# Another order, with its engines and buffers, for the same pieces of an attention and MLP kernel

## The chip, the cores and the metric

The kernel runs on one core of one Trainium2 chip. The metric is the device time in microseconds (us) of one execution. The kernel before takes 614.69 us, the median of three runs (613.73 to 614.74).

## What is computed

```python
q, k = rotate(q), rotate(k)                      # rotary embedding, (4, 8, 576, 64)
scores = (1 / sqrt(64)) * q @ k.T
attn = exp(scores - max(scores)); attn = attn / (sum(attn) + 1e-9)
x = (attn @ v) as (2304, 512)                    # tokens x heads*64
h = x @ w_in                                     # (512, 2048)
out = (s * relu(h) ** 2 + b) @ w_out             # (2048, 512)
```

All inputs are of type float32; the weights are stored as 64-bit words and are turned into 32-bit numbers on the chip.

## The kernel before

The 32 heads are treated as 16 pairs (`NPAIR`), four of them for each of the four batches. Of each pair, q, k and v are loaded, q and k are rotated (`rotate`, three tensor-tensor steps each, lines 592, 594 and 596), scaled, split into two 16-bit parts (`qk_hi`, `qk_lo`, `v_hi`, `v_lo`) and transposed. The first four pairs (`FQ`) skip the split and are worked on in 32 bits. The scores of 128 rows form one tile: TensorE writes it to PSUM (`s_tile`, lines 675 and 676, or `s_pair`, line 657), VectorE takes the row maximum straight from PSUM (`s_max`, line 681), ScalarE the exponential (`s_exp`), and the normalised result is split into two halves `pab` (`p_a`, a scaled cast, and `p_b`, line 407). A DMA transposes `pab` into `pt` (`p_t`, line 739), and TensorE multiplies with v (`pv_sum`, line 760).

The 32 weight tiles are converted in four steps each (`w_sign`, `w_low`, `w_rebias`, `w_join`), and their largest column sums are taken (`w_gram`, line 478). Later they are split into two 16-bit halves in place (`w_hi`, `w_lo`). The MLP goes in nine units (`NU`). Unit 0 works in 32 bits (`mlp_in0`, line 913, `mlp_out0`, line 930), the others in three 16-bit products (`mlp_in`, line 887, `mlp_out`, line 963). A unit from 1 on begins with its norm: `x_norm` on ScalarE, two additions `x_add` (line 846), the matmul `x_sum` (line 852, one for each unit), then `x_scale`, `x_hi` and `x_lo`. After each first product come relu and square on ScalarE and a split into `g_hi` and `g_lo` (line 905). Unit 7 (`NU - 2`) is the last: its second half of rows is summed in two column halves, and `out_sum` and `store` follow for each of its three parts. Line 511 (`bias_cols`, 32 matmuls in a row) stands once in the program.

`plan()` lists 2691 pieces with what each reads and writes, and for some pieces the engines that may do them. Three tables of characters then fix everything else. `ORDER` gives the order in which the pieces are written, and so the order of every engine's queue. `PICKS` gives the engine of each piece that has a choice (G is GpSimd, S is ScalarE, V is VectorE). `SLOTS` gives the buffer that each new tile takes, of the few that `BUFS` allows (two for scores in PSUM, four for loaded weights, six for `pab`, two for `pt`). Each engine works through its queue in order, and all loads, transposes and stores stand in one queue, that of SyncE (SP). The loop that does it:

```python
for n in order:
    x = work[n]
    ...
    if x["pick"]:
        a = (*a, pick[x["fn"], a])
```

In the profile GpSimd is called POOL, VectorE DVE, ScalarE ACT and TensorE PE. Most VectorE and ScalarE steps go through helpers, so their line is that of the helper: 402 and 404 for a tensor-scalar step, 407 for `scalar_tensor_tensor` on VectorE, 410 for ScalarE.

Of the kernel before, what the change touches and what calls it, by code (L numbers as in the profile page):

```python
# [35 lines left out]


ORDER = (
    "AJADAGAFAEAHAKAMALANAOAIAPDUAADfEBECDgEDEEDhEFEGAdAeAfAgDVDWDkDTD_AhDcEHDdA3EADeDiEIA4EJDXA5DYDlESELDZDrDjA6A7EMEKJjJkEN"
# [3 lines left out]
    "EtK6KCBOBhLBJzLCKRFIBJBPE3BgFTBQBfFUKLBmEwKMBiK7BlLDB4B6B7KWBcBWKXKeCSACBnKDKSLEBoE4LFKEKYKZB5KaB8K8KfKTFhB-KbBjBpKnCVKg"
    "CUBqKhKvKoKwK9CTKcB_BdCWKdKiETClCLKUB9KjKpKqCBKVFVEqK-CACCKrKkLJCoLKLRFQKlCmKxCnLLKsKmLMKycdCMLSCNLTCpCOKzEUKtCPLNLrCDbM"
    "bObLLGCYK_FHCsCybNLULsCELVLWCZCaF7LHLOLtbPCbbQLICzC1LaLPK0CcbRExbSCXCdbTLXLQLuFkCuCvLiLbEyEzE0CtLcE1CwE-LdcecfcgCeLechE_"
    "ciMRLvFRLwLjC0LkLfMSLlC2CFC_DADBDCbWbVLYMTCICHLZLmE8bYF6L3bXK1KuCfCGLgL4MUbZbaL5F9DDMVcjCgCibhbgK2bfDMLnLxMEDODNMFCJLoLh"
# [39 lines left out]
PICKS = (
    "VSSGGGVSSGSSGSSGSSVSSGSSVVSGSSVSSGSGVSGGSSVVSVSGGSSGSSVSSGSSGSSVSSGSSGSSGSGGSSVSSGSGGSSGGGGGGGGSVVSSSVVSSSVVSSSVVSSSVVSS"
    "SVVSSSGVSSSVVSSSVVSSSVVSSSVVSGGVVGSVVVSSVGVGSGVVSVGVGGSSSSSVGSVGSSGSSGSSVSVGSSVSSSSSVGSGVSSGSSSSSVSSSSSGVSSSVSGVVSSGSSSS"
    "SSVSSSSSSSSSGGSSVSSSSGSSSSSSSSSSVSSSGSSSSSSSSSSSSSVVSSSGVSSSVSVSSVSVSSVVSVGVSGSSVSSSVSSSSSSSGSSSVVVVVSSGVSSSGSSSVSVGVSGG"
    "VGVSSSSSSGVSSSVSSVSSVVGVVVVVVSGVSGGVVGVVVVGVSSVSSVVGVSVVSSSSSSSSSGGSSGSSGSSGVSSVGSGSSGSGSVVSSVSGSGSVSGSGSVSGVSSGSVSVSGSG"  # L90
    "VVSGSVVVVGSGVGSVVGVGSGSGVSVVSGVGSVSVSGVVSGVVVVSVSVVGSVSGSVVVVVSVSVSGSGSVVGVGSGVVVGSGVVVGVVSVVVSVVVVGSVVGVVVGSGSGVV"
)

SLOTS = (
    "010000121000113110001201101002001331101011111210100101202011230001130011100330101010011021210131000112301100201031000121"
    "110131010323100010011223110113234005000101001201001112013401001312102101110500100031103241100310211030011000001303232140"
    "101412101013153012014011001101231020111130011054301130001001100112103122101540203010201100100013011031305400221101123301"
    "310010012401001113000011023110010020101053100120320101100110200111023300111010021001000510123101022112111300013110101104"
    "020200101200201103150010124011311210021031110011002510121100011230011010241101320050032110312010022000011130120010010101"
    "314111001011023502110002210013030410110005102011032001101001104220100001233115010013100121001301130014221111020113010105"  # L100
    "331000031010111500123010242010110103110000521421030100101242502102101100011201103130100112020030112330540011113001103120"
    "011321520121030040011201311003100200110013251402103120100013011010201012010002110210101254001002011310131012000012130110"
    "00221112000110020003013100110102111003201211001001311120100000101110210110001201010"
)


# [987 lines left out]
```

## Time and profile before

| | before |
|---|---|
| median of three runs | 614.69 us |
| span of the profiled execution, first to last instruction | 611.0 us |
| what lies around the span, against the median | 3.7 us |
| PE busy | 584.1 us, 96% of the span |
| DVE busy | 473.7 us, 78% |
| ACT busy | 412.8 us, 68% |
| POOL busy | 122.7 us, 20% |
| SP queue (loads, transposes, stores) | 63.9% of the 16 DMA engines' time |

The share of busy time is an average over stages: the profile's second part, which cuts the span into 40 slices, shows PE at 2 and 6 tenths in the first two slices and at 9 from the third to the last but one, and DVE at 8 or 9 from the second slice to the twentieth but between 1 and 6 in the last nine. So the stages have to be read one by one.

### The profile page before, as it was taken

The numbers are of one execution on the slowest core, as the hardware profiler recorded it, in microseconds if no ns is written. First come the engines' busy times: TensorE is split into PE (matmuls) and PEld (weight loads), VectorE is DVE, ScalarE is ACT, GpSimd is POOL, SyncE is SP. The second block draws the span as 40 slices with busy tenths as digits, with TensorE's granted clock in tenths as the row PEclk, the third lists the DMA queues.
The fourth block names the chain that finished last, engine by engine and source line by source line (L and its number), as shares of the span: only waits on it lengthen the run. The fifth ranks groups of instructions, "written<-read, shape, count | busy, mean of one in ns | idle before, by whom it ended". The sixth has DMA issues, their size and how long they took to land.

```text
span 611.0 us, 12423 instructions
## 1 busy us (share of the span) xinstructions
PE 584.1 (96%) x4658; PEld 394.5 (65%) x4658; DVE 473.7 (78%) x1037; ACT 412.8 (68%) x864; POOL 122.7 (20%) x130
## 2 busy tenths in 40 slices
PE   2699999999999999999999999999999999999997
PEld 1466777566676657665765676657675766766875
DVE  5999998989999999999978879898777536533212
ACT  3599988778989998877677858568544534623322
POOL 2122334310111211111232322210110212010100
PEclk9999999899999999999999999999999999999999
DMA  8787999599774599978686976765681120361100
GB/s 317 274 279 233 282 231 220 121 201 196 181 160 92 95 198 232 188 139 197 151 150 106 179 178 131 145 145 108 142 170 26 30 74 1 79 155 36 36 1 34
DMA packets 210012, 90.32 MB, mean 148 GB/s; under 512 B 192288, under 2 KB 196768, under 8 KB 209952
## 3 DMA queue, kind: packets, MB, share of 16 engines
q1 hardware_dynamic: 209952, 89.54, 63.9%
q8 instruction: 36, 0.59, 0.4%
q14 instruction: 24, 0.20, 0.1%
HBM read 31.97 MB, written 4.72 MB: 60 GB/s over the span
## 4 chain that ended last, share of the span: by engine, by line
PE 77%; ACT 8%; DMA 6%; DVE 5%; issue 2%; POOL 1%; SPq 1%; ACTq 0%; DVEq 0%
PE px L887 25%; PE po L963 24%; PE px L760 8%; PE s L675 7%; PE po L930 4%; PE px L913 3%; DMA pt<-pab 3%; PE s L963 2%; PE s L657 2%; DVE s L681 2%; DMA x<-in_moe_w_out_dram 2%; ACT wio L410 1%; ACT p L410 1%; ACT x L410 1%; DMA x<-in_moe_w_in_dram 1%
## 5 line engine op out<-in xcount | busy, mean ns | idle before, releaser
L887 PE MATMUL px<-xa,wio 128*128 128x256 f16 x1536 | 182.2, 273 | 0.0
L963 PE MATMUL po<-wio,g 128*128 128x512 f16 x720 | 176.2, 379 | 0.0
L887 PEld LDWEIGHTS <-wio 128*128 128x128 f16 x1536 | 148.1, 98 | 33.5 <-issue 2.6
L410 ACT ACTIVATE p<-s,nm 128x576 f32<-128x576 f32 x144 | 105.6, 735 | 60.4 <-DVE s L681 52.2
L407 DVE SCALAR_TENSOR_TENSOR pab<-p,sum,pab 128x576 f16<-128x576 f32 x136 | 115.6, 866 | 9.5 <-POOL pab L404 8.1
L963 PEld LDWEIGHTS <-g 128*128 128x128 f16 x816 | 75.5, 98 | 66.5 <-issue 2.5
L681 DVE TENSOR_SCALAR_CACHE_REDUCE s<-s,sc 128x576 f32<-128x576 f32 x108 | 87.0, 819 | 17.5 <-PE s L676 17.1
L410 ACT ACTIVATE hr<-px,xc 128x512 f32<-128x512 f32 x64 | 43.5, 680 | 79.6 <-PE px L887 77.9
L905 POOL TENSOR_TENSOR g<-hr,g 128x512 f16<-128x512 f32 x35 | 42.5, 1215 | 183.6 <-DVE g L784 75.7
L410 ACT ACTIVATE pab<-p,sum 128x576 f16<-128x576 f32 x75 | 55.8, 764 | 5.0 <-DVE sum L709 3.5
L760 PE MATMUL px<-pt,v 128*64 128x320 f16 (+2 forms) x640 | 50.2, 281 | 2.8 <-DMA pt<-pab 2.7
L404 POOL TENSOR_SCALAR pab<-p,sum 128x576 f16<-128x576 f32 x28 | 24.0, 859 | 114.4 <-DVE sum L709 69.8
L410 ACT ACTIVATE hr<-hr 128x512 f32<-128x512 f32 x68 | 42.6, 627 | 1.6
L760 PEld LDWEIGHTS <-v 128*64 128x64 f16 x640 | 33.5, 110 | 15.5 <-issue 8.9
L675 PE MATMUL s<-qkT 128*128 128x512 f16 (+1 forms) x120 | 41.6, 383 | 0.0
L675 PE MATMUL s<-kS,qkT 128*128 128x512 f16 (+1 forms) x120 | 41.5, 380 | 0.0
L675 PEld LDWEIGHTS <-qkT 128*128 128x128 f16 (+1 forms) x240 | 22.2, 100 | 26.4 <-issue 6.5
L784 DVE CAST g<-hr 128x512 f16<-128x512 f32 x23 | 10.1, 438 | 37.7 <-ACT hr L410 23.4
L913 PEld LDWEIGHTS px<-x,wio 128*128 128x128 f32 x256 | 30.6, 192 | 3.9 <-issue 2.9
L905 DVE TENSOR_TENSOR g<-hr,g 128x512 f16<-128x512 f32 x29 | 19.8, 686 | 17.1 <-ACT g L410 16.9
L913 PE MATMUL px<-x,wio 128*128 128x128 f32 x256 | 32.6, 280 | 0.2 <-DVE wmx L481 0.2
L404 POOL TENSOR_SCALAR wio<-x 128x512 bf16<-128x512 f32 (+1 forms) x25 | 22.4, 898 | 51.3 <-ACT x L410 25.2
(146 smaller groups left out, 865.0 us busy)
## 6 DMA issues: line engine op xcount, KB each, us to landing
x<-in_moe_w_in_dram SPq DMA_DIRECT2D x16, 512.0 KB, 4.2
x<-in_moe_w_out_dram SPq DMA_DIRECT2D x16, 512.0 KB, 4.7
st_v<-in_v_dram SPq DMA_DIRECT2D x16, 320.0 KB, 4.4
st_q<-in_q_dram SPq DMA_DIRECT2D x16, 288.0 KB, 3.5
st_k<-in_k_dram SPq DMA_DIRECT2D x16, 288.0 KB, 3.6
out_dram<-o SPq DMA_DIRECT2D x7, 512.0 KB, 3.1
kS<-qkT SPq DMA_DIRECT2D x24, 144.0 KB, 2.7
pt<-pab SPq DMA_TRANSPOSE x152, 3.0
```

The lines of the kernel that those rows point to most:

```text
L404: eng.tensor_scalar(out=out, in0=in0, scalar1=s1, scalar2=s2, op0=op0, op1=op1)
L407: nc.vector.scalar_tensor_tensor(out=out, in0=in0, scalar=scalar, in1=in1, op0=op0, op1=op1)
L410: nc.scalar.activation(out=out, in_=in_, func=func, **kw)
L657: nc.tensor.matmul(ps[h][:, to], d["qF"][hh, t * P:(t + 1) * P], d["kF"][hh, keys], start=True, stop=True)
L675: nc.tensor.matmul(ps[rows, MAIN:2 * MAIN], lhs, kk[:, h:8:2], start=(n == 0), stop=(n == 1))
L681: nc.vector.tensor_scalar(out=T["s"], in0=T["s"], scalar1=-1.0 / 8.0 if pr in FQ else st[pr]["es"], scalar2=None, op0=ALU.mult, op1=ALU.mi ...
L760: nc.tensor.matmul(o[64 * h:64 * h + 64, c], v_rows(pr, h, k, z), p_rows(pr, 2 * (i // 4) + h)[:, k, c], start=((z, k) == todo[0]), stop=( ...
L887: nc.tensor.matmul(ph, w16[0][:, f, wz, cc], X["xa"][:, xz, c], start=(c == 0 and n == 0), stop=(c == NC - 1 and n == 2))
L905: (nc.vector if eng == DVE else nc.gpsimd).tensor_tensor(out=g[:, 1], in0=r, in1=g[:, 0], op=ALU.subtract)
L913: nc.tensor.matmul(ph, wi[:, f + 1, c * P:(c + 1) * P], xs[0]["x"][:, c, j * P:(j + 1) * P], start=(c == 0), stop=(c == NC - 1))
L930: nc.tensor.matmul(X["po"][:, j * DM:(j + 1) * DM], gs["h", j, f - f % 4][:, f % 4 * P:(f % 4 + 1) * P], wo[:, f + 1], start=(n == 1), sto ...
L963: nc.tensor.matmul(po, g[:, gz, jj], w16[1][:, f, wz, to], start=(n == 1 and i == 0), stop=(n == NF and i == 2))
```

## The change

Nothing is computed in another way: the same 2691 pieces are written in another order, some of them on another engine, with other buffers. Only the three tables differ. They come from a search that takes VectorE's steps between SBUF operands and GpSimd's steps as excluding each other. The first row of each table:

```diff
 ORDER = (
-    "AJADAGAFAEAHAKAMALANAOAIAPDUAADfEBECDgEDEEDhEFEGAdAeAfAgDVDWDkDTD_AhDcEHDdA3EADeDiEIA4EJDXA5DYDlESELDZDrDjA6A7EMEKJjJkEN"
+    "AJADAdAADUDTAwAMALAKANAFAOAqAGD_AeAfAEEAAHAgAIA3AhEBAPAWDfDgDcDdAzDhAyAxDkDeAsA0AtDiEIA9ArEJDjDpAuDlELAQA5JjDVEKA6A4AYAX"
...
 PICKS = (
-    "VSSGGGVSSGSSGSSGSSVSSGSSVVSGSSVSSGSGVSGGSSVVSVSGGSSGSSVSSGSSGSSVSSGSSGSSGSGGSSVSSGSGGSSGGGGGGGGSVVSSSVVSSSVVSSSVVSSSVVSS"
+    "VSSVGSGSSGSSVSSGSSVSSVSSVSSGSSGSGVGGGVSGGSGSGVGSGSSGSSGSSGSGGSSGGSGGGGSSVGSGGSGSSVGSGSSGSGGGSGSGVVSSSVVSSSVVSSSVVSSSVVSS"
...
```

Pieces by engine, where the numbers differ (a rotation counts as one, with three instructions; an `x_add` with two):

| piece | VectorE | GpSimd | ScalarE |
|---|---|---|---|
| rotate | 29 to 24 | 3 to 8 | |
| p_a | 33 to 22 | 28 to 39 | 75 to 75 |
| g_hi | 23 to 17 | | 41 to 47 |
| g_lo | 29 to 26 | 35 to 38 | |
| x_add | 8 to 4 | 0 to 4 | |
| qk_hi | 1 to 1 | 4 to 11 | 19 to 12 |
| w_low | 2 to 1 | 4 to 10 | 26 to 21 |
| w_hi | 3 to 1 | 9 to 7 | 20 to 24 |
| w_sign | 11 to 10 | 21 to 22 | |
| w_rebias | | 8 to 7 | 24 to 25 |
| x_hi | 5 to 3 | | 3 to 5 |
| p_diag | 2 to 0 | 5 to 3 | 1 to 5 |
| p_s | 29 to 24 | | 59 to 64 |
| v_hi | 2 to 3 | 3 to 3 | 11 to 10 |

TensorE has the same pieces in both, and so has SP.

The first place is the start of VectorE's queue, before it:

```order
L402 TENSOR_SCALAR wio<-x_110 128x512
L407 SCALAR_TENSOR_TENSOR wio<-x_110,wio 128x512
L407 SCALAR_TENSOR_TENSOR wio<-x_108,wio 128x512
L481 TENSOR_REDUCE wmx<-px_120 128x1
L592 TENSOR_TENSOR z_134<-st_q_130,tab 128x9x2x32
L594 TENSOR_TENSOR st_q_130<-st_q_130,tab 128x576
```

The same place in the changed kernel (`x` are loaded weights, `wio` converted ones, `tab` the table of the rotation):

```order
L402 TENSOR_SCALAR wio<-x_108 128x512
L407 SCALAR_TENSOR_TENSOR wio<-x_108,wio 128x512
L402 TENSOR_SCALAR wio<-x_112 128x512
L402 TENSOR_SCALAR wio<-x_110 128x512
L407 SCALAR_TENSOR_TENSOR wio<-x_110,wio 128x512
L407 SCALAR_TENSOR_TENSOR wio<-x_112,wio 128x512
L481 TENSOR_REDUCE wmx<-px_127 128x1
L592 TENSOR_TENSOR z_156<-st_q_116,tab 128x9x2x32
L594 TENSOR_TENSOR st_q_116<-st_q_116,tab 128x576
```

Ahead of the first rotation there stand now three more steps on VectorE, those of a third weight tile and one that GpSimd did; that tile's load stands ahead of the table's on SP.

The second place is GpSimd's queue in the stretch before the norm of unit 1, before the change (`z`, `st_k` belong to a rotation, `nat` to `qk_hi`, `pab` to `p_a`):

```order
L404 TENSOR_SCALAR x_1193<-x_1193 128x512
L592 TENSOR_TENSOR z_1412<-st_k_1334,tab 128x9x2x32
L404 TENSOR_SCALAR pab_1485<-p_1464,sum_1347 128x576
L594 TENSOR_TENSOR st_k_1334<-st_k_1334,tab 128x576
L404 TENSOR_SCALAR pab_1596<-p_1521,sum_1520 128x576
L596 TENSOR_TENSOR st_k_1334<-st_k_1334,z_1412 128x576
```

And in the changed kernel:

```order
L404 TENSOR_SCALAR nat<-st_k_570,sc 128x9x64
L592 TENSOR_TENSOR z_1540<-st_q_1450,tab 128x9x2x32
L594 TENSOR_TENSOR st_q_1450<-st_q_1450,tab 128x576
L596 TENSOR_TENSOR st_q_1450<-st_q_1450,z_1540 128x576
L404 TENSOR_SCALAR pab_1623<-p_1549,sum_1489 128x576
L592 TENSOR_TENSOR z_1693<-st_k_1574,tab 128x9x2x32
L594 TENSOR_TENSOR st_k_1574<-st_k_1574,tab 128x576
L596 TENSOR_TENSOR st_k_1574<-st_k_1574,z_1693 128x576
```

GpSimd does two whole rotations where it did one, and a cast of `nat` that ScalarE did.

The third place is the end of VectorE's queue, before the change (`o` and `hr` hold the three parts of unit 7):

```order
L905 TENSOR_TENSOR g_7756<-hr_7750,g_7756 128x512
L407 SCALAR_TENSOR_TENSOR o<-po,xc,bcs 128x512
L407 SCALAR_TENSOR_TENSOR hr_7797<-s_7556,xc,bcs 128x256
L407 SCALAR_TENSOR_TENSOR hr_7810<-s_7549,xc,bcs 128x256
L1089 UNCONDITIONAL_BRANCH
```

And in the changed kernel:

```order
L784 CAST g_7756<-hr_7744 128x512
L407 SCALAR_TENSOR_TENSOR hr_7786<-s_7515,xc,bcs 128x256
L407 SCALAR_TENSOR_TENSOR hr_7797<-s_7520,xc,bcs 128x256
L407 SCALAR_TENSOR_TENSOR o<-po,xc,bcs 128x512
L1089 UNCONDITIONAL_BRANCH
```

The part with 512 columns was summed and stored first of the three, and is now the last.

## Rows read from the trace of the kernel before

**Rows 1.** The page, parts 1 and 2: busy us, then tenths in 40 slices

```profile
PE 584.1 (96%) x4658; PEld 394.5 (65%) x4658; DVE 473.7 (78%) x1037; ACT 412.8 (68%) x864; POOL 122.7 (20%) x130
DVE  5999998989999999999978879898777536533212
```

**Rows 2.** Busy time by stage: stretch, its us, then each engine's busy us

```profile
8.20:38.40 30.20, 20.97 (x116) 14.34 (x116) 27.91 (x64) 19.42 (x35) 7.46 (x8) 1.00 0.85 300
38.40:91.10 52.70, 50.41 (x499) 37.16 (x498) 50.87 (x127) 48.75 (x113) 15.80 (x22) 1.00 0.91 252
91.10:164.60 73.50, 70.57 (x506) 46.56 (x503) 67.69 (x150) 59.90 (x134) 17.38 (x19) 0.98 0.87 182
164.60:223.60 59.00, 59.00 (x479) 39.01 (x481) 58.00 (x120) 54.89 (x113) 10.16 (x12) 1.00 0.66 139
223.60:470.00 246.40, 245.56 (x2007) 160.06 (x2007) 213.17 (x462) 174.97 (x377) 49.86 (x46) 1.00 0.74 151
```

**Rows 3.** Timeline of PE at five places: start us, us, what

```profile
24.20 1.11 PE L767 MATMUL s<-ident,st_k 128*128 128x128 f32 x4 [0.79 <-ACT p L410]
...
39.15 0.60 PE L767 MATMUL s<-ident,st_k 128*128 128x128 f32 x4
...
91.11 1.16 PE L913 MATMUL px<-x,wio 128*128 128x128 f32 x8
...
164.59 0.27 PE L852 MATMUL px<-g,ones16b 128*128 128x256 bf16 x1
...
223.55 1.91 PE L511 MATMUL px<-wio,ones 128*32 128x512 f16 x32
```

**Rows 4.** The chain that ended last, two pieces in a full stretch: start, us, what

```profile
411.17 9.17 PE px L887 x84
...
485.21 4.53 PE po L963 x21
```

**Rows 5.** Timeline of DVE, start of its queue and two steps in a row

```profile
5.96 0.75 DVE L402 TENSOR_SCALAR wio<-x 128x512 uint16<-128x512 uint16 x1 [4.79 <-ACT x L410]
...
9.45 0.75 DVE L592 TENSOR_TENSOR z<-st_q,tab 128x576 f32<-128x576 f32 x1
...
14.55 0.76 DVE L596 TENSOR_TENSOR st_k<-st_k,z 128x576 f32<-128x576 f32 x1
15.22 0.75 DVE L592 TENSOR_TENSOR z<-st_k,tab 128x576 f32<-128x576 f32 x1
```

**Rows 6.** Groups by form: x count, busy us, mean ns of one

```profile
L402 DVE TENSOR_SCALAR pab<-p,sum 128x576 f16<-128x576 f32 x33 | 18.0, 545 | 0.4
L404 POOL TENSOR_SCALAR pab<-p,sum 128x576 f16<-128x576 f32 x28 | 24.0, 859 | 114.4 <-DVE sum L709 69.8 <-ACT g L410 14.4 <-DVE sc L404 9.2
L407 DVE SCALAR_TENSOR_TENSOR pab<-p,sum,pab 128x576 f16<-128x576 f32 x136 | 115.6, 866 | 9.5 <-POOL pab L404 8.1 <-ACT pab L410 0.9
```

**Rows 7.** Timeline around a rotation on POOL: DVE's steps, then POOL's

```profile
347.69 0.80 DVE L407 SCALAR_TENSOR_TENSOR pab<-p,sum,pab 128x576 f16<-128x576 f32 x1
...
349.14 0.82 DVE L681 TENSOR_SCALAR_CACHE_REDUCE s<-s,sc 128x576 f32<-128x576 f32 x1
...
354.30 1.96 DVE L407 SCALAR_TENSOR_TENSOR pab<-p,sum,pab 128x576 f16<-128x576 f32 x1
...
349.07 1.15 POOL L905 TENSOR_TENSOR g<-hr,g 128x512 f16<-128x512 f32 x1
...
354.13 1.50 POOL L596 TENSOR_TENSOR st_q<-st_q,z 128x576 f32<-128x576 f32 x1
```

**Rows 8.** Who waited for whom: us in total, times, longest

```profile
ACT p L410 <- DVE s L681: 52.2, 37, 7.3
```

**Rows 9.** Last sum on DVE, and DMA issues by size: KB, us to landing

```profile
607.57 0.48 DVE L407 SCALAR_TENSOR_TENSOR hr<-s,xc,bcs 128x256 f32<-128x256 f32 x1 [1.15 <-PE s L963]
...
out_dram<-o SPq DMA_DIRECT2D x1, 256.0 KB, 2.5
out_dram<-hr SPq DMA_DIRECT2D x2, 128.0 KB, 1.9
```

More of the change, by code (lines that the diff above doesn't have):

```diff
@@ L43 @@
[L43 to L46, printed above, removed]
@@ new lines @@
+    "KCBbKKKDLAK6BmCSE3LBKLE5B6BlK7BnE4KWKMBoLCJzB5B-B7KSKXEpCTKEKeKYBJB8KfBPBpCUBQBjClKZKgKnKTEtKaCVK8KhLDBqKbKiK9CWKcLEB_Ko"
+    "CYFIK-KUKdLFKpCBKvBWBcCAKjCmBdKwCCKVDoLJCLKkK_CbFTB9KxCZCaLKKlCnLRLLCcCoLGLrFULMKmLSCpbLCsEwKyCNLNCyLsCDLTbMLOLUE6LVCMbN"
+    "CECOLPbOKzCPLtLHLWC_bPK0LaLQLubQcdEULICvCdCtceLXCXLvLiCubRC0cfCeLjbSCwKqExbTKrcgCFEyKschEzE0FHciE1E7LwMRFhKtLkC1LYE-LlCz"
+    "LmMSE8bVK1EqcjbWLZFQKuMTbYCGLbMUDBE_bXLcE9bgLdbZFfLeLnL3F6baC2CIckK2DMLfDAL4CHbhLoDCMVMEK3L5bfLgABbiLxMFLhCJC3MWL0DDC5bj"
@@ new lines @@
+    "MXbkCxFAbUMCF9L1bbMDFVL2LpCfMGMHC4L6FkMIMdLyL7LqMJL8b0GHL_LzC6Mqb1FiMLMeFKMKb2DPMMMfb3DNL9C7MNFLM3FRb4MAb5bcMrM4MBbdFMFS"
+    "M5CKFNL-GICQM6C8MaFOCgFPM7C9M8b6FYMoDGCiF7b7ChMbDOFBCRbeMcDQDEMgC-M9MOMhCjMpFZMlMiDFFgNADJMYMmclMsbqMjMnDIMtNObsMxDHNBMu"
+    "blMkMyNPbpcmNCMZbrGJcnDKMPMzNDMQMvbtbuFqCkMwCqFjbmFWNQFtNEDLNRDRbnDSNSNFNTboFXNUFuNmCrNGF5FCFadDNHNLcoM0FvNncpN0F-NXNINM"
+    "Flb8M-FmN1b9FnNJFoNVNoNdNKFpM2cqFccAM_NeM1cBcrFrNfNNb-FsF8NYNpFyGENgNZNhNib_NqNWNjdENrbvGFNsbwcCNtFDN2NxbxFzN3ODcsGUcDOG"
@@ new lines @@
+    "GGFbOEN4NaN5OHN6ctNuN7cENccuN8N9F2dFcFcvdGNyOFNkcGdHdINbNvOUOINzcIcwOJGXFwOVF_ORNwcxcKN-OWGAcLGBOKNlOSOOOLcJcyOTN_GCOhFx"
+    "czOkcMGhcHF0cNOMOXcTGDc0OYcVOiOZFdOcc1OaOAOjc2Olc3cOF1OPOmOdcPOnOBOCFEOydwOeOvOoOzcUGKdxOwONO0cQdyc4OxdzcSGTGMd0O1c5d1GN"
+    "O_cWP7c6GucXbyGVd2GLc7cROpO2d3Gtc8O3GOcYd4d5d6O4d7cZc9PAcaOQd8PBcbGQc-PCcceIObP8c_O6OqbzeHF3GWOsPDdAPEd-GPO7dBGePQeJd9dC"
+    "eKP9OtOfPFd_dJdKeAFeeBeROudLeCeLdMPNOrP-PGeDF4dNeFPHdOGveEO8P_PRdPQAeGOgPOPKeSGYO5dQPPPIemdRGiGxPrPLeTeleMeUPSdSeOGfdTPd"
@@ new lines @@
+    "enGgGZeNPTeoGaQBePepGbebPUGcPsPVGyGdPWPtO9dUGkPeeVdVPgPYPXeqecPfeWPhGwGRdWeQedPZPuO-eYdXG7PaeaeeG8e6efdYPJPiegPve5PjPMGj"
+    "PwPkGSeXPxe7QHPyGldZGzeZP2daehPzG0QIdbejPodcQEeie8P3PlPbP0e9GmQFQJekPmPcP1QGesGnddeuPpP4QKQSdeQVPqQLewQTdfQPQMdgPnevQUQW"
+    "G1QXG2erHIG3G9HJdhQsG4HHetQYexQZdifEeyQtdjezQQe-QdP5dkQae0dlfDQeP6fQdmQfe2Qbdne4fRfFQDe1fSHLQNfAfGdoQOfTQvfHfUdpfVQuQwfI"
+    "QRQxG5QjQCHVHMQ9fWdqQkfCQcG6drQlfXfYe3HWQmGodsQ6QnHKfZQ-e_fafBHXfbQyQgQzQ7QofcQ_fJGpQhQpQifLduQ8RUQqG-HNfdRAHARBRFQrQ3HO"
@@ new lines @@
+    "RCHPRVRzfeHQRDQ0R0RWREfKHSG_fffMHRfgQ4RXfyQ1Q5HTRYfxHhdtRZHURGdvR1RiRaQ2fofzRbRfRjf0RHfhRlHBfnRkf1fiRcHCgQHEfpfNfqRmgPHi"
+    "frRgHFR2RLR3RdR4RIfsRMRnRNRofOR_HYRpRhRqSKf2HkfjRrRJfPfkgRHsSLHjflgSHDftHlfvRtSMfmRKRORPR8RugTgGRQR9gURvR-gFRRRsHaHtSAHe"
+    "SNf8RSSBgHSCHZfuRTHbfwReSsR5f7SDSOSEHcHvSPf4Stf3f9SQSFf5f-H8Hmf6f_H7gASuSbRwScgISHgJSRHdSSSISpRxgKSGRygaSVSqSWSrgBSTSXHn"
+    "SvSeSwgZHoSxHuHpSfSJH_gCGqS0HwgDR7SgHGgLSdgEHxSUgMHqHrShH0SiTHSmR6S1gOSjgWSyGrgbS5SnHygkIJS6gcHfgdTISYH9TJIKS8HzSaSzS7gN"
@@ new lines @@
+    "H1SZgVH4S9gwH2gjILS-gxgygYH-geS2TKSkglgzgggmg0giH5g1IAg2S_g3gXg4gnTAg5TLgfSlgoToTMghGsIvTNTEIBgqSog6g7TlTOgpg8IXgsJKTPIC"
+    "grTpg-IDTQIGg9IEIFguTFS3g_TmhAHghBhITBgtS4IHhHTnIITqTaTCTrhJhShCTbTDJNIyTSTXTGhEhKI6hRhLTsTTH3IaJXhmTwTRTthlhMhTI7TUhUIM"
+    "TYhDhnhGINTZhFTxhvhoJYTcT4TdTeJZTiTVT5hpT6TuhwTWTyTjhVTfhqT1TvUDTghxhbhWUEThhyT2hOTkhQI8T3hYH6UFhaIVT7IOT8T9hcIPT-UGIWhN"
+    "UHhPUIhXhZUJhdUKUOU7heUPUTUAhfTzULhgIZUBhhU8IjUChjUUU9h5UQUMU-T0hzU_UcUVT_h0h6IkUdIYUNUfUeUWUXhiVAUgh7VVIlh8hkVWhsIgVXhr"
@@ new lines @@
+    "UYh9huUZIbURIcUhIdIhUiUjIeUkhtIfVBUaUSUtUliEiQUuUmiRUqUviDUriSIQh-UsiTh1iUUwh3iViWiXVHiYiZiaVSUxVIibh2Unh4U1UoiAiFicUph_"
+    "iGiCiHU2iBUbVJiIVTidU3VUUyVEVYieVZVFVaUzinifVbU0VGiKVKigVLgvioIoVMIRIpVdVjipVeIxWLIwU4VkWMVliqiJVcWNirV9isWOixU6U5ihVDIi"
+    "VmiiV-V6VfiLImiMVNVCjFVPV7VOiyiNWPInjGWQiOizJJJLVQi0ikIzVnVRVoimV_VpiuV8I9IqVvjHi7I-I0VwijWAVxWBWFiljIWGVsJMitWRjJWiWCi8"
+    "IrWjJUVtWkVgVujKVyVzWDiwViVqVhV0WlV3jZi1WHi9i2ivi-WmWEi3V4Wni5V1V5I1W_WoWUWpWtjaVrI2i_XAjAi4V2XBI3i6I4WVjbjCI5WuWWWXI_jc"
@@ new lines @@
+    "jPWYJCWqWzWZJAWIW0WaWrWbWcW8WKWsW1jEW9WfjQWdWJJOJBWejMjdWgX1jRjBW2WvJDjSjjW3W-W4jeWhX2XyXCjDXDXzXEWTjLW5X0jkJVWSX3jOX4jl"
+    "JEX5X9JPXnjTXFXNjmjNX-JWWwXoXOXpXHXPjUXbJFJQWxXIjVjwIsjWiPjYWyjxISJRjyjXITjzjgjnj0jij1joXJjfj2j3XKJSj4JTj5W7Jajqj6JcXLj7"
+    "jhItjpXMj8jrXQW6jsXRJdXSXkj-juXGXVjtj9XWXTXXkRj_JbkAXcXUkSkBXlX6kCJekIXdkTXeJgYaIUkUkDkVX7kHXmYbXqXYXfIukJJfkKXrXskLXtYD"
+    "XZXvkEkMYEXuXakGYcXgkOXhYFX_YdkWYGkFYeXjYMYHYfkQYNk5X8YgXwYhYiYlkNXiYIJGYPYJk6XxYOYQkcYRJHk7YSYTYmY3k8ZTYUkbYVZUYAY4ZVYj"
@@ new lines @@
+    "YXZFkdYWYYkYYCY5ZGkaYZYBJIY0kekmY1YKY2klYnkfY6Y7Y_ZCZAkvYkY8ZDkgkPZEYLkXZHkZjvknZIZJkhJhZNkokjZOZKYrkpYoYsY9YtZLkwYqY-Yp"
+    "YuYvJiYwZWZMk9a7YxlDkqYyZXkxkikyZBkkZYksZZYzkzkrZaa8ZblEZea9ZPk0ktaCZflFk1k-aDlGZkkuaEZlk3ZcZmZQk2ZRZdlQZhk4lRk_lHlSZilB"
+    "ZSlIlTlAlUojlClVlWlXZja-lYoklKlZZnlalbZxlMollcomlJlLonooleopZooqlOZsorlNZpldoslPotZqlxlfa_ZrlgoulybAZybBloZtlzlhZul0bCli"
+    "Z0Zzl8Z1ZgbGl1aSl2lnovljlpl7bHZ2lllqlkZ3l9Z4atZ8Z5Zvl-lrbDlslmaTltbElulvZ9aUmFZ6ZwauZ7mGZ-lwmHl4mIZ_avmJmamKaAmQaBmPaFl_"
@@ new lines @@
+    "aGaHaIl3mRmAaJl6mSaKl5aLmBmTaMmZmUmCmbmEmMmOaPagmWahmjaQaRmDmLaVmcaWmYaamdmkaimemNmladaXmVaemmowmnabmomXmgaYoxmfoymhafmp"
+    "ajozakmralpEo0amo1mimqmsaNmumtaopFacawanpGo2axpHo3aOapmvo7aZpIpJo6aqpOo8aypPo9aza0a1o-o5a4pjpQa5pRo_pia2o4pkpAplpBpDpCar"
+    "pKasa6pSpMpTpLbFpNpsa3pYbIpZpVpapXpbpUpmpcpWpdptpnbJpupebKmwpgpopvmxpfphmypppwmzpqpxprm0m1p3m2m3m4m5m6m7pzp1m8p2pyp4nJp5"
+    "p6p0p7nKm-nLnMp8nNp9m9nVm_nAp-nBniqAnCp_nOnhqBqCnDnjnFnknEnGnlnInmnRnUnWnHnXnQnTnYntnZnanPnSncnbn5n6nun7n8nfnvnenwnonnnx"
@@ L84 @@
+    "oSnynqoFoGnrnzn2ndngnpn9nsn0oHn-n1n4oIoRoJoKn3oTn_oUoAoDoVoMoBoWoEoNoCoQoZocoPofoYoboLoeoOohoXoioaodog"
 )
 PICKS = (
[L87 to L89 removed]
@@ L100 @@
[L100 to L103, printed above, removed]
+    "012003001110201010300101011010020311030102011100112000010101100123103032211001031110100100103112002101213010100030011301"
@@ new lines @@
+    "301001101010201000103101013234310010001101015100010100112011001103201010301100321041005001123110020010012011030242001011"
+    "531110110010240112221310021110130100510141300110020302100101140301211112202230001010100000113513301300120020300001211002"
+    "104111031111000015200112001000021311113520401102101005030011001230200110001113100100111042000000131501101001131001221214"
+    "212001030003010050000211202131310001121110000300112510130101402120131400002011310031310112011121500031011001021431010021"
@@ L104 @@
+    "000311113001002141110250111132000000210100310311210015010240010101010301131012011101331100102040101013302200011100310201"
+    "101200034110510112020010100010423121005001010111000122150111001201241121021120001004310003101430111100312032205003311010"
+    "120312133001401311020001150143212320202011100010104311020102110121011120025101010100011210011030001531001100101201421011"
+    "00120030013212004011001101000210100211000100210311102100011100101201101000110210010"
 )
```

54 lines of the change are left out of this document (7 added, 47 removed).

## The prediction

> **What bounds the kernel now.** The page says PE, with 96% of the span [rows 1]. The table of busy time by stage tells where the rest goes [rows 2]: PE is busy for 20.97 of 30.20 us up to 38.40, 50.41 of 52.70 up to 91.10, 70.57 of 73.50 up to 164.60, and from there to 470 it lacks less than 1 us in 305. Busy is not yet full speed: four transposes of line 767 take 1.11 us at 24.20 and 0.60 at 39.15 [rows 3]. That is half the rate, the lower of the clock's two levels (1.2 and 2.4 GHz), though the clock column says 1.00 for that stretch.
>
> So I counted PE's work. Each piece in PE's queue counts with the time from its start to that of the piece behind it when nothing is awaited, as read after 40 us: 0.109 us for a matmul of line 887 (84 in 9.17 us), 0.216 for one of line 963 (21 in 4.53 us) [rows 4], the other kinds in the same way. All 708 pieces make 567.8 us, in both orders, since PE's pieces are the same. The span is 611.0, so 43.2 us are lost. The place of a matmul tells how much was lost until then: 13.2 us of work stand ahead of the transposes at 39.15, so 25.9 are lost; 60.7 ahead of the eight matmuls of line 913 at 91.11 (lost 30.4); 128.4 ahead of line 852's first at 164.59 (36.2); 187.3 ahead of line 511 at 223.55 (36.3) [rows 3]. From there to the end of PE's work 3.5 us are added and behind it 3.4. Whatever the new order brings, it has to come out of these 43.2 us, and most of them lie before 91.
>
> What holds PE there is VectorE above all: 27.91 busy of 30.20 us, then 50.87 of 52.70, 67.69 of 73.50 and 58.00 of 59.00 [rows 2]. ScalarE is nearly as busy from 38 to 91 (48.75 of 52.70), but waits 52.2 us for VectorE's row maxima [rows 8].
>
> **VectorE's queue.** I counted it in the same way, with start-to-start times (0.67 us for a step of a rotation, whose own duration is 0.76 [rows 5]), up to the last step that a given matmul of PE needs. Ahead of the transposes at 39.15 stand 27.0 us before and 26.7 in the new order; ahead of the eight matmuls of line 913 71.0 and 66.6; ahead of line 852's first 139.0 and 126.9; ahead of line 511 195.3 and 186.9. PE's own work ahead of them is 13.2 and 13.9, 60.7 and 60.7, 128.4 and 129.3, 187.3 and 186.8. The 8.4 us at line 511 are seven rotation steps fewer (59 to 52, 4.7 us), four casts of `p_a` (4 to 0, 1.7), two `s_max` (60 to 58, 1.5), two `w_hi` (3 to 1, 1.0) and small steps (1.4), less two `g_lo` and one `p_b` more (1.9). At line 852 it is 12.1, as `p_b` and `v_lo` that stood ahead of it come behind it in the new order.
>
> **The start.** VectorE's first rotation begins at 9.45 with four steps done since 5.96 [rows 5]; in the new order seven stand ahead of it, 1.3 us more work in the same time if the rotation's data come at the same time. A 512 KB load stands ahead of them now, 1.7 us at the 300 GB/s of this stretch [rows 2]. I take 1.3 us gained; the bounds are 1.3 gained and 0.4 lost.
>
> **What GpSimd takes over, and what it costs.** It has 18.3 us ahead of line 913 and 23.0 in the new order, 38.5 and 52.0 ahead of line 852, 49.5 and 64.5 ahead of line 511. It is slower at these steps (a cast of `p_a` 859 ns against 545 [rows 6]), which costs nothing by itself while it idles four fifths of the span [rows 1]. But its steps hold up VectorE's. A `p_b` takes 0.80 us alone and 1.96 beside a rotation step on POOL, while an `s_max`, which reads PSUM, takes 0.82 beside a POOL step [rows 7]. The 136 `p_b` take 866 ns in the mean, 66 over the free 0.80, together 9 us for 122.7 us of POOL [rows 6, 1]; the other kinds of steps roughly double it, so up to 0.2 us of VectorE for each us of POOL. With 4.7 us more of POOL ahead of line 913 that is 0.9 us; with 13.5 more ahead of line 852 it is 2.7, so that VectorE's lead there is 9.4 and not 12.1.
>
> The Trainium skill's SBUF — State Buffer, section Who interferes with whom, says that a VectorE instruction with two SBUF inputs contends with a GpSimd instruction that reads SBUF, and that one with at most one SBUF input and outside the 2-port modes does not; [rows 7] agree with both halves. Its Perfetto Trace Analysis, section Optimizing Scalar/DVE Operations, warns that moving work between these two might not help. That speaks against this change; what it would make of the time is the slower rival below, whose price is from rows.
>
> **The sum**, against the median of 614.7 (the profiled span plus 3.7 around it; every term is a difference):
> - Until line 913: VectorE is the bound, its queue is 4.4 shorter, less 0.9 for POOL: -3.5. PE can follow, since it had lost 25.9 by 39.15, and 30.4 less 3.5 is 26.9. Bounds: 0 and -5.7 (with the start).
> - From there to line 852: before, 5.8 us are lost. VectorE's queue ahead of this matmul is 9.4 us shorter (5.9 of them beyond the term before), so waits on it should go; others stay (data to land, ScalarE, a stretch at the lower clock about 110 us, which the mean of 0.98 shows [rows 2]). I take half: -2.9. Bounds: 0 and -5.8.
> - From line 852 to the end of PE's work: 3.5 us lost before. Half, for the same reason: -1.6. Bounds: +1 and -3.5.
> - The end: the last part is now the one of 512 columns. Its store takes 2.5 us to land against 1.9 for a half, and its sum 0.75 or so against 0.48 [rows 9]: +0.9.
>
> Together -7.1, so 607.6 us. The further steps on GpSimd behind line 511 I cost at nothing: PE is full there (245.56 of 246.40 us up to 470, with DVE at 213.17 [rows 2]), and DVE is at 7 to 9 tenths until the 31st slice and at 6 or fewer behind it [rows 1]. If that cover were gone, they would cost up to 0.2 us of VectorE each, as above.
>
> **Rivals.**
> *ScalarE becomes the bound.* Its queue hardly shrinks: 66.8 and 65.9 ahead of line 913, 124.2 and 122.4 ahead of line 852. For it: 48.75 busy of 52.70 [rows 2]. Against it: its waits for VectorE [rows 8]. Then the first two terms are -0.9 each, the third 0, the end +0.9: 613.8.
>
> *GpSimd holds VectorE up (slower).* In the new order VectorE has 126.9 us ahead of line 852, and POOL 52.0. Before it was 139.0 plus 0.2 times 38.5, 146.7. If each us of POOL costs VectorE r us, the new order is later from r = 0.38 on. At r = 0.5 it is 6.2 us later there, and with the end +0.9 the time is 621.8; at r = 1, 648. For it: steps of a rotation on POOL read two operands and stand in chains of three, eight of them instead of three, and one of them more than doubled a `p_b` [rows 7]. Against it: the rate of before is half of 0.38, and VectorE's `s_max` and other PSUM steps, over a quarter of its queue, can run beside POOL.
>
> *More waits go than I count.* If the start gains its 1.3 us, and PE's dense stretch (two transposes and three products in a row without VectorE steps between) comes earlier, the matmuls run at the full rate earlier than about 38 us. Then: -5.7, -4.5, -2.5 and +0.9, so -11.8: 602.9.
>
> **Chances.** Forecast 0.53 (605 to 611), ScalarE 0.17, GpSimd 0.16, more gained 0.14. The range from 601.5 to 616.0 takes in all but the larger part of the GpSimd case and a little of the last. A measurement of this kernel can tell about 0.2%, 1.2 us, from no change. Faster by more than that: the forecast, the last, and a little of ScalarE's, 0.72. Within it: most of ScalarE's, 0.12. Slower: GpSimd's, 0.16.
>
> **What would show it.** In the new profile the eight L913 matmuls that now begin at 91.11 begin at 87 to 88 us, L852's first at 159 to 160 and L511 at about 217. DVE is busy some 20 us less in all and POOL some 50 us more. The four transposes that took 0.60 us begin near 37 to 39. A `p_b` mean of over 1.0 us would show the GpSimd rival; DVE with idle time before 160 us and ACT full would show ScalarE's. What would make me wrong: a late load at the start, or a chain of small steps (`x_add` on GpSimd for four units) that PE waits for.

## The result, and the profile of the changed kernel

The changed kernel takes 620.03 us (619.81 to 620.31, four runs) where the kernel before took 614.42 in the same comparison: a ratio of 1.0095, interval 1.007 to 1.012. It is 5.6 us slower; the forecast was 7.1 us faster. The two profiled executions differ by 7.2 us (spans of 618.2 and 611.0), so sums made on the traces come out 1.6 us larger than the times. Where the time and the span of an execution are both on record, they differ by 1.7 to 2.1 us; so the profiled execution of the kernel before took about 612.8 us (an estimate), and the 3.7 us "around the span" hold this difference to the median too.

First the parts 1 and 2 of the page, to be read beside [rows 1] (busy us, then tenths in 40 slices):

```profile
PE 583.5 (94%) x4658; PEld 394.4 (64%) x4658; DVE 474.4 (77%) x982; ACT 416.6 (67%) x873; POOL 194.5 (31%) x176
...
DVE  6999998999999999799998888978877752412102
```

VectorE has 55 instructions fewer and is busy for as long as before. GpSimd is busy 71.8 us more. The table by stage answers [rows 2], with the same bounds:

```profile
8.20:38.40 30.20, 21.84 (x132) 14.78 (x132) 29.05 (x63) 20.61 (x39) 9.30 (x8) 0.94 0.88 321
38.40:91.10 52.70, 48.91 (x499) 37.60 (x501) 50.33 (x119) 48.63 (x116) 26.17 (x28) 1.00 0.95 239
91.10:164.60 73.50, 72.28 (x511) 46.90 (x508) 68.97 (x152) 61.44 (x135) 30.32 (x28) 1.00 0.91 187
164.60:223.60 59.00, 58.35 (x492) 37.95 (x491) 58.70 (x117) 53.63 (x113) 14.22 (x14) 1.00 0.67 136
223.60:470.00 246.40, 237.55 (x1929) 156.47 (x1928) 213.30 (x427) 168.10 (x364) 87.58 (x69) 0.99 0.71 150
```

The last line holds the result: PE, which was full from 223.6 to 470 (245.56 of 246.40), now lacks 8.85 us there, while DVE is as busy as before (213.30 and 213.17) and POOL went from 49.86 to 87.58. Ahead of it PE is earlier. The timeline of PE at the places of [rows 3] (start us, us, what; the eight matmuls that began at 91.11 are the second eight of the 24 in the second row and begin at 88.66):

```profile
37.08 0.66 PE L767 MATMUL s<-ident,st_k 128*128 128x128 f32 x4
...
87.66 2.94 PE L913 MATMUL px<-x,wio 128*128 128x128 f32 x24
...
159.52 0.27 PE L852 MATMUL px<-g,ones16b 128*128 128x256 bf16 x1 [0.52 <-ACT sum L410]
...
217.61 1.91 PE L511 MATMUL px<-wio,ones 128*32 128x512 f16 x32
```

With PE's work ahead of each place (13.9, 60.7, 129.3 and 186.8 us) the loss of the prediction's counting is 23.2, 28.0, 30.2 and 30.8 us, where it was 25.9, 30.4, 36.2 and 36.3. Then it turns: by the end of PE's work the changed kernel has lost 46.2, the one before 39.8. So 15.4 us are lost behind line 511, against 3.5.

How they are lost is seen around 235 us, where the loss first grows by over 1 us (DVE, then POOL, then ACT, then PE):

```profile
231.65 1.96 DVE L407 SCALAR_TENSOR_TENSOR pab<-p,sum,pab 128x576 f16<-128x576 f32 x1
233.54 0.81 DVE L681 TENSOR_SCALAR_CACHE_REDUCE s<-s,sc 128x576 f32<-128x576 f32 x1
...
235.42 1.35 DVE L407 SCALAR_TENSOR_TENSOR sc<-sc 128x1 f32<-128x1 f32 x1
...
231.60 1.40 POOL L592 TENSOR_TENSOR z<-st_k,tab 128x576 f32<-128x576 f32 x1
233.08 1.80 POOL L594 TENSOR_TENSOR st_k<-st_k,tab 128x576 f32<-128x576 f32 x1
234.96 1.80 POOL L596 TENSOR_TENSOR st_k<-st_k,z 128x576 f32<-128x576 f32 x1
...
239.06 0.74 ACT L410 ACTIVATE p<-s,nm 128x576 f32<-128x576 f32 x1 [3.28 <-DVE s L681]
...
239.94 0.38 PE L675 MATMUL s<-qkT 128*128 128x512 f16 x1 [1.99 <-ACT p L410]
...
240.43 2.46 PE L887 MATMUL px<-xa,wio 128*128 128x256 f16 x12
```

A rotation runs on GpSimd in three steps. Beside them a `p_b` takes 1.96 us instead of 0.80 (below, such a longer step is called held), and a step on a single column, which takes 0.15 us elsewhere, ends together with GpSimd's third step, 1.35 us after its start. The `s_max` at 233.54, which reads PSUM, keeps its 0.81. Behind these the next row maximum is late, ScalarE waits 3.28 us for it, and PE waits 1.99 for ScalarE. In the 10 us ahead of PE's wait VectorE is busy for 9.97, in the 10 us ahead of the next wait of over 1 us (at 283.77) for 9.96. Ahead of the third (at 332.97) it is busy for 8.76 only; there two of its steps are held: a cast takes 1.64 us (438 ns in the mean before) and a `p_b` 1.96 (three stretches, columns as in [rows 2]):

```profile
229.90:239.90 10.00, 7.89 (x66) 5.57 (x64) 9.97 (x17) 3.86 (x9) 6.70 (x5) 1.00 0.47 109
273.80:283.80 10.00, 8.51 (x69) 4.97 (x67) 9.96 (x17) 6.90 (x15) 5.81 (x5) 1.00 0.66 152
323.00:333.00 10.00, 7.82 (x74) 4.62 (x72) 8.76 (x14) 5.12 (x12) 3.75 (x2) 1.00 0.24 68
```

I compared each VectorE step with the median of its kind in the kernel before. In all they are 42.9 us longer, against 19.9 before; from 217 to 470 us 26.8 against 10.4. Shared out over the GpSimd steps that they overlap, the 18 rotation steps of that stretch account for 15.8 us (0.88 each, for steps of 1.79 in the mean), 22 `g_lo`, which also have two SBUF operands, for 8.4 (0.38 each), 20 `p_a`, which have one, for 1.5 (0.08 each). A rotation step that stays on VectorE costs 0.67. By this sharing the six rotations cost VectorE more on GpSimd than they cost when it does them itself.

Another way in which they could do harm is to come late for the steps behind them. The trace speaks against it: these are the waits of other engines for GpSimd that the changed kernel's trace shows (us in total, times, longest), and none is for a rotation.

```profile
DVE pab L407 <- POOL pab L404: 4.1, 5, 1.2
ACT hr L410 <- POOL g L905: 1.7, 2, 1.1
```

### The profile page after: what moved, and what is told of

Read it like the earlier page. It is cut to its first block, busy times and chain, and to the rows that moved or that the text cites. A ratio compares the mean times of both kernels' runs of the same rounds, so it can differ in the third digit from the quotient of the medians.

```text
span 618.2 us, 12465 instructions
## 1 busy us (share of the span) xinstructions
PE 583.5 (94%) x4658; PEld 394.4 (64%) x4658; DVE 474.4 (77%) x982; ACT 416.6 (67%) x873; POOL 194.5 (31%) x176
## 5 line engine op out<-in xcount | busy, mean ns | idle before, releaser
L963 PE MATMUL po<-wio,g 128*128 128x512 f16 x720 | 173.5, 379 | 1.0 <-DVE g L784 0.9
L410 ACT ACTIVATE p<-s,nm 128x576 f32<-128x576 f32 x144 | 105.5, 733 | 62.4 <-DVE s L681 50.8
L407 DVE SCALAR_TENSOR_TENSOR pab<-p,sum,pab 128x576 f16<-128x576 f32 x136 | 127.1, 947 | 7.4 <-POOL pab L404 4.1
L681 DVE TENSOR_SCALAR_CACHE_REDUCE s<-s,sc 128x576 f32<-128x576 f32 x108 | 87.4, 818 | 16.1 <-PE s L676 15.9
L905 POOL TENSOR_TENSOR g<-hr,g 128x512 f16<-128x512 f32 x38 | 50.3, 1327 | 149.9 <-ACT g L410 103.7
L410 ACT ACTIVATE hr<-px,xc 128x512 f32<-128x512 f32 x64 | 43.6, 681 | 71.4 <-PE px L887 67.9
L404 POOL TENSOR_SCALAR pab<-p,sum 128x576 f16<-128x576 f32 x39 | 36.3, 932 | 113.1 <-DVE sum L709 95.2
L410 ACT ACTIVATE pab<-p,sum 128x576 f16<-128x576 f32 x75 | 56.1, 765 | 10.6 <-DVE sum L709 6.2
L404 POOL TENSOR_SCALAR wio<-x 128x512 bf16<-128x512 f32 (+1 forms) x32 | 33.1, 1042 | 44.4 <-DMA x<-in_moe_w_in_dram 17.5
L410 ACT ACTIVATE hr<-hr 128x512 f32<-128x512 f32 x68 | 42.6, 626 | 1.4
L675 PEld LDWEIGHTS <-qkT 128*128 128x128 f16 (+1 forms) x240 | 22.1, 100 | 24.8 <-issue 5.3
L410 ACT ACTIVATE g<-hr 128x512 f16<-128x512 f32 x47 | 29.4, 625 | 10.1 <-PE s L963 6.7
L676 PEld LDWEIGHTS <-qkT 128*128 128x128 f16 (+1 forms) x240 | 22.0, 101 | 15.5 <-issue 10.4
```

The source lines that it names most:

```text
L404: eng.tensor_scalar(out=out, in0=in0, scalar1=s1, scalar2=s2, op0=op0, op1=op1)
L407: nc.vector.scalar_tensor_tensor(out=out, in0=in0, scalar=scalar, in1=in1, op0=op0, op1=op1)
L410: nc.scalar.activation(out=out, in_=in_, func=func, **kw)
L675: nc.tensor.matmul(ps[rows, MAIN:2 * MAIN], lhs, kk[:, h:8:2], start=(n == 0), stop=(n == 1))
L676: nc.tensor.matmul(ps[rows, MAIN - TAIL:MAIN], lhs, kk[:, 8, 64 * h:64 * h + 64], start=(n == 0), stop=(n == 1))
L681: nc.vector.tensor_scalar(out=T["s"], in0=T["s"], scalar1=-1.0 / 8.0 if pr in FQ else st[pr]["es"], scalar2=None, op0=ALU.mult, op1=ALU.mi ...
```

## The experiments

**The late rotations alone, from both sides.** Theory A: GpSimd's steps with two SBUF operands, the rotations above all, hold VectorE up and so PE. Rival B: the new order behind line 511 is at fault. The first edit is to the changed kernel; the second kernel is the one before with the same lines and `POOL`.

```diff
             pick[x["fn"], x["a"]] = {e[0]: e for e in ENGINES}[next(engs)]
+    for a in ((10, "k"), (11, "k"), (12, "q"), (13, "q"), (15, "q"), (15, "k")):
+        pick["rotate", a] = DVE
```

> The changed kernel, with the six rotations that stand behind line 511 on GpSimd put back on VectorE; order, buffers and all other engines as changed. Theory A (GpSimd's rotation steps hold VectorE up: 18 steps of 1.79 us there go with 15.8 us by which VectorE's steps are longer, 0.88 each, while a step taken over saves VectorE 0.67): VectorE is busy some 4 us less in all although it does 12 us more work, p_b is shorter than 947 ns in the mean, the waits of PE between 217 and 410 us shrink from 12 us to 6 or fewer, 611 to 616 us. Rival B (the new order itself leaves PE too little lead behind line 511, whatever the engine): 619 to 624, and VectorE busy up to 12 us more.

It took 616.17 us where the kernel before took 614.62 on the same chip, a ratio of 1.0028 (1.0007 to 1.0049) against the changed kernel's 1.0095: 4 of the 5.6 us are gone. The time lies just above A's range, which had put more on the rotations.

The changed kernel's `p_b` first, then this run's page:

```profile
L407 DVE SCALAR_TENSOR_TENSOR pab<-p,sum,pab 128x576 f16<-128x576 f32 x136 | 127.1, 947 | 7.4 <-POOL pab L404 4.1
...
PE 579.7 (95%) x4658; PEld 392.9 (64%) x4658; DVE 470.9 (77%) x1000; ACT 416.7 (68%) x873; POOL 162.3 (26%) x158
...
L407 DVE SCALAR_TENSOR_TENSOR pab<-p,sum,pab 128x576 f16<-128x576 f32 x136 | 119.4, 890 | 7.2 <-POOL pab L404 3.9
```

VectorE does 18 steps more (12 us) and is busy 3.5 us less (470.9 against 474.4); a `p_b` takes 890 ns in the mean, against 947 in the changed kernel and 866 in [rows 6]. PE loses 9.8 us behind line 511, not 15.4. That bears A out in the main, and it leaves 6 us more than the 3.5 of before. The profiled execution took 614.58 us, 1.6 less than the median; so the rotations are worth 5.6 us by the traces and 4 by the times.

> The kernel before, with the same six rotations on GpSimd (one of them was there already, so 15 steps move). Theory A: VectorE loses 10 us of work and its other steps get 13 us longer, so its busy time rises by 2 to 5 us from 473.7; PE waits in a few places that it did not, 615.5 to 620 us. Rival B: VectorE is relieved and the order is good, so 613 to 614.5.

615.83 us against 614.62, ratio 1.0026 (1.0006 to 1.0045): slower by 1.6 us by the ratio (1.2 between the medians), at the lower end of A and outside of B. VectorE's busy time rose to 475.7 with 10 us less to do:

```profile
PE 584.7 (95%) x4658; PEld 395.1 (64%) x4658; DVE 475.7 (77%) x1022; ACT 413.1 (67%) x864; POOL 147.3 (24%) x145
```

In the old order the same six rotations cost less than the 4 us of the new one, so the order has a part in it.

**Steps that nobody needs.** To measure the hold by itself, 36 idle steps were added to the kernel before, behind line 511 (two behind every second GpSimd piece), once with two operands, once with one:

```diff
+                    for _ in range(2):
+                        nc.gpsimd.tensor_tensor(out=extra, in0=tab[:, 0:5, 0:64], in1=tab[:, 0:5, 32:96], op=ALU.mult)
```
```diff
+                        nc.gpsimd.tensor_scalar(out=extra, in0=tab[:, 0:5, 0:64], scalar1=2.0, scalar2=None, op0=ALU.mult)
```

> The kernel before, with 36 idle steps added on GpSimd behind line 511, two behind every second of 18 GpSimd pieces: products of two SBUF operands of 128x320 float32 into a tile that nobody reads. VectorE's own work is as before. Theory A (a GpSimd step with two SBUF operands holds VectorE's up for about half of its time, one with one operand for a fifth or less): some 30 us more POOL, VectorE busy 10 to 15 us longer, and since VectorE's slack behind line 511 is small, 617 to 623 us. Rival D (what counts is GpSimd's time, of whatever kind, at 0.2 of it): VectorE 6 us longer.

> The same 36 idle steps at the same places with one operand (a scaled copy of the same 128x320 float32 elements into the same tile). Theory A: some 18 to 20 us more POOL, VectorE busy 1.5 to 4 us longer, 614 to 616 us. Rival D: the same rate for each us of POOL as the run with two operands.

The parts 1 of both pages and their steps (with two operands first; the lines of the kernel are one higher here):

```profile
PE 587.3 (94%) x4658; PEld 397.2 (64%) x4658; DVE 487.3 (78%) x1037; ACT 413.3 (66%) x864; POOL 162.9 (26%) x166
...
L1026 POOL TENSOR_TENSOR extra<-tab 128x320 f16<-128x320 f32 x36 | 40.5, 1124 | 1.4
```
```profile
PE 584.5 (94%) x4658; PEld 396.2 (64%) x4658; DVE 476.9 (77%) x1037; ACT 413.8 (67%) x864; POOL 163.6 (26%) x166
...
L1026 POOL TENSOR_SCALAR extra<-tab 128x320 f16<-128x320 f32 x36 | 42.6, 1183 | 1.5
```

GpSimd is busy with the added steps for nearly the same time, 40.5 and 42.6 us. VectorE, whose own work is that of before (473.7), is busy 13.6 us longer with two operands and 3.2 with one: 0.34 and 0.08 us for each us of GpSimd. Rival D, one price for all of GpSimd's time, falls. The times are 626.18 and 619.97 against 613.03 (ratios 1.021, 1.0176 to 1.0245, and 1.0107, 1.0075 to 1.0139). Both are slower than I expected: the steps with one operand cost 6.9 us, although they hardly hold VectorE. From 223.6 to 420 us PE's matmuls wait 2.4 us for `pt` and 1.5 for `g` (before, 0.8 and 0). GpSimd's own pieces come later behind the added ones; the 1.5 us end with a `g_lo` of VectorE that takes 1.62 us beside a rotation step put off in this way. That the rest of the 6.9 us has the same cause is argued, not shown. So GpSimd's idle time was not free either.

**The front and the rest apart.** The order of one kernel up to a piece, and the other's order of all pieces that are left, on the engines of the kernel that each part comes from. The tables differ from one piece on, so only the numbers of pieces are given. Rival C: PE loses behind line 511 because it comes there early, whatever follows.

> The changed kernel's order and engines up to and with line 511 (1136 pieces), and behind it the other pieces in the order and on the engines of before; buffers dealt anew. Theories A and B alike (what is won ahead of line 511 stays won when the rest is as before): 608 to 610 us. Rival C (the 6 us won there cannot be kept, since PE then arrives early at data or at buffers that are late in any order): 613 to 616.

616.04 us, ratio 1.003 (1.001 to 1.005). The time misses A and B and lies at the upper end of C's range, but the trace puts the loss at the splice: PE has lost 32.0 at line 511 (36.3 before), then 7.2 within 20 us, and 3.6 in all that follows. The two orders don't join there (the row is PE's first wait behind line 511, for ScalarE's exponential):

```profile
223.79 0.42 PE L675 MATMUL s<-qkT 128*64 128x512 f16 x2 [3.13 <-ACT p L410]
```

> The changed order and engines for the first 1040 pieces (a place ahead of line 511 where the queues of the two orders join with a shorter wait), behind them the rest as before; buffers dealt anew. Theories A and B: PE is 5 us ahead of before when it comes to the splice, loses 2 to 3 there, and behind it no more than before (3.5 us): 611 to 613. Rival C (what is won ahead cannot be kept in the rest of before): 614 to 616, with waits spread over the rest.

With a splice 96 pieces earlier it took 610.45 us against 613.03, ratio 0.996 (0.9943 to 0.9977): faster than both kernels. PE has lost 30.9 where it had lost 36.0 before (at 150 us of its work), gives 3.5 of it back at the splice, and loses 4.4 behind line 511. So a part of what the front wins is kept, and the rest of before loses hardly more behind it than it did (3.5): C falls.

> The reverse: the order and engines of before up to and with line 511 (1142 pieces), behind it the changed ones; buffers dealt anew. Theories A and B: the whole loss of the rest, 12 us, less what the earlier front gave, so 624 to 627 us. Rival C (PE loses behind line 511 only because it comes there 6 us earlier): 618 to 621.

623.68 us, ratio 1.0161 (1.0137 to 1.0185): just below the range of A and B and above that of C. PE comes to line 511 with 36.4 lost, as before, and loses 13.3 behind it. The changed rest is slow by itself; it takes no early PE to make it so.

**The order with the engines of before.**

> The changed order and buffers with every piece on the engine that it had before. VectorE has 25 us more work than in the changed kernel, GpSimd 51 us less. Theory A: VectorE's other steps are 20 us or more shorter than in the changed kernel, so that it is busy within 3 us of 474; the front is a few us later than in the changed kernel, the rest loses less: 614 to 619. Rival B (the order is what costs): the rest loses its 12 us again, 620 or more.

638.95 us, ratio 1.0423 (1.0394 to 1.0452): far outside of A's range.

```profile
PE 586.9 (92%) x4658; PEld 394.9 (62%) x4658; DVE 487.5 (77%) x1037; ACT 413.0 (65%) x864; POOL 139.3 (22%) x130
```

Every piece is on the engine that it had, and yet VectorE is busy 487.5 us against 473.7: the order alone puts other steps side by side, and VectorE's steps are 34.5 us longer than the medians, not 19.9. Line 511 comes at 230.58 us, 13 later than in the changed kernel, and behind it PE loses 19.6 us. My expectation took the hold to follow GpSimd's work; it follows from the order too. So the new order is not good for the old engines, and B is right to this degree: order and engines can't be priced apart.

**What is left of the loss behind line 511.** Two further edits on top of the late rotations on VectorE: seven `g_lo` back on VectorE, chosen by the longest holds, and, in the other run, 22 casts `p_a` behind line 511 given to GpSimd.

```diff
+    for a in ((1, 12), (2, 8), (3, 4), (4, 12), (4, 14), (5, 4), (6, 4)):
+        pick["g_lo", a] = DVE
```
```diff
+    for a in ((5, 7), (6, 5), (6, 6), (6, 7), (7, 6), (11, 0), (11, 3), (8, 8), (8, 5), (10, 8), (10, 7),
+              (11, 7), (11, 6), (12, 8), (13, 3), (13, 8), (14, 2), (14, 8), (15, 1), (15, 3), (13, 6), (14, 7)):
+        pick["p_a", a] = POOL
```

> The changed kernel with the six late rotations on VectorE, as in the run before with these, and seven pieces g_lo (two SBUF operands) also back on VectorE: those seven by which VectorE's steps were 0.8 to 1.2 us longer each, more than the 0.61 that such a step takes on VectorE. Theory A (what is left of the loss behind line 511 is these holds): VectorE is busy 2 us less than with the rotations alone, PE's waits behind line 511 shrink from 9.8 to 7 or 8, 613 to 616 us against the changed kernel's 620.0. Rival B (what is left is the order): the time stays within 1 us of the run with the rotations alone.

> The changed kernel with the six late rotations on VectorE, and in their place 22 casts p_a (one SBUF operand) behind line 511 moved from VectorE to GpSimd: VectorE's own work is 2.5 us more than in the changed kernel, GpSimd's steps in the rest take some 17 us less. Theory A (one-operand steps hold VectorE for a tenth of their time): VectorE is busy 7 to 8 us less than with the rotations alone, so PE waits less than 9.8 us behind line 511: 613 to 616 us. If GpSimd's slower casts come late for the p_b behind them, VectorE sits idle for them and the gain is lost: 616 to 620.

With the `g_lo` it took 614.56 against 613.96, ratio 1.0012 (0.9996 to 1.0028), which the interval does not separate from 1.0028 of the rotations alone. VectorE is busy 469.6 (1.3 less), and PE loses 9.4 behind line 511 instead of 9.8. By the trace these holds are no more than 0.4 us of what is left; the time cannot tell, as 614.56 lies in the ranges of both A and B. With the casts it took 616.89, ratio 1.0054 (1.0034 to 1.0075): VectorE is busy only 461.5, 9.4 less, as a step with one operand hardly holds it, but PE loses 11.1. The waits of VectorE say why (engine and line waited for: us in total, times, longest):

```profile
DVE pab L407 <- POOL pab L404: 13.9, 16, 1.6
```

These were 3.9 us with the rotations alone. VectorE now stands still for GpSimd's slower cast where it had worked, which is the second case of the expectation.

## Why the prediction was wrong

The front was won about as forecast, but in part in another way; the step that failed is the third term of the sum, with the sentence that costs GpSimd's further steps behind line 511 at nothing.

- **Until line 913**: forecast -3.5, measured -2.4 in the loss (30.4 to 28.0). The size came near, but not by VectorE's shorter queue, from which the term was made. 2.7 us are already gained at the transposes (25.9 to 23.2), where that queue is 0.3 shorter; from there to line 913 PE loses 4.8 us where it lost 4.5, although the queue gets 4.1 shorter. The early gain goes with two things that the sum left out. One is the start, which gave what was taken for it: VectorE's first rotation begins at 9.37 with seven steps done, where it began at 9.45 with four. The other is the clock: four transposes took 0.63 us at 30.41, near the 0.60 of full speed, where the kernel before still needed 1.11 at 32.04. This is the condition of the third rival, though the granted clock then fell once more (0.94 in the mean up to 38.40). What each of the two gave is not shown. The rows (the changed kernel's DVE and PE, then PE before):

```profile
9.37 0.75 DVE L592 TENSOR_TENSOR z<-st_q,tab 128x576 f32<-128x576 f32 x1
...
30.41 0.63 PE L767 MATMUL s<-ident,st_q 128*128 128x128 f32 x4
...
32.04 1.11 PE L767 MATMUL s<-ident,st_k 128*128 128x128 f32 x4 [0.21 <-ACT qkT L410]
```

- **A row misread**: ScalarE was set aside between 38 and 91 us since it waits 52.2 us for row maxima [rows 8]. These are the waits of the whole run; from 38.40 to 91.10 they are 0.7 us (`ACT p L410 <- DVE s L681: 0.7, 1, 0.7`). ScalarE is as busy there in the changed kernel (48.63 of 52.70 us) as before, and that it kept PE from gaining in this stretch is possible, but no run shows it.
- **From line 913 to line 852**: forecast -2.9, measured -3.6 (the loss between the two places went from 5.8 to 2.2). Together the two terms are -6.0 against -6.4, in part by luck. The two places came at 88.7 and 159.5 us where 87 to 88 and 159 to 160 were named, and line 511 at 217.6, named as about 217.
- **From line 852 to the end of PE's work**: forecast -1.6 with bounds of +1 and -3.5, measured +12.4. This is the step that failed. The further steps of GpSimd were put at nothing behind a cover: PE's 245.56 of 246.40 us and VectorE's 213.17. Both are shares over 246 us. VectorE's 33 us of idle time, as many after as before, lie elsewhere for the most part: in the 10 us ahead of each of PE's first two waits of over 1 us it has less than 0.1, ahead of the third 1.2. What the runs showed in place of free steps is a loss of 15.4 us behind line 511 against 3.5, of which the six rotations alone make 4 to 5.6. A full PE proves that nothing was late with the old steps, not that there is room for longer ones.
- **The price of a us of GpSimd**: forecast up to 0.2 us of VectorE, taken from a mean over all its steps. Measured 42.9 us for 165.7 of work, 0.26 (before, 19.9 for 114.3, 0.17); for what the change adds, 23.0 us for 51.4, which is 0.45 and more than twice the price that was taken. The prediction's 0.38, from which on the change was to lose, is a price for all of GpSimd's work ahead of line 852, so it compares with the 0.26: by that sum the change had to win up to there, and it did. The sentence of [rows 7] on a rotation step that more than doubled a `p_b` showed it; the mean over the `p_b` in [rows 6] hid it: 111 of the 136 met no GpSimd step and took 0.81 us, 24 overlapped one by over 0.1 us and took 1.12. The new order makes them 45, at 1.22.
- **The slower rival** was the right mechanism in the wrong place: not ahead of line 852, where it was priced and where VectorE's steps with two operands met few rotations (6 steps, 2.6 us), but behind line 511. Its 621.8 at half a us for each us lies near the 620.0 by luck, as it counts a loss ahead of line 852 where there was a gain.
- **The end**: forecast +0.9, measured +0.8 (from the end of PE's work to the end of the span 4.2 us against 3.4).
- **The views named to judge by**: POOL was to be busy some 50 us more and was by 71.8, as its own steps got longer too; DVE was to be busy 20 us less and was not. A `p_b` mean of over 1.0 us was named as the mark of the rival; the change lost with 0.947.
- **What stays open**: of the 12 us that are lost behind line 511 beyond those of before, the rotations are 5.6 by the trace (4 by the times), and the seven `g_lo` no more than 0.4. The other 6 show, for the larger part, in the run with the rotations on VectorE as waits of about 1 us each at five places (four for the exponential, one for `pt`), with VectorE busy for 9.0 to 9.9 of the 10 us ahead of each. That the order packs VectorE's steps too densely there is argued, not shown; the run with the engines of before says only that the order counts.
